# Attention beside a weight product: the first scores moved to the end of the product's first half, seven slots a unit

## The chip, the core and the metric

One core of a Trainium2 chip runs the program. TensorE (PE) multiplies, VectorE (DVE), ScalarE (ACT) and GpSimd (POOL) work element by element, and SyncE (SP) issues most of the DMAs. Each engine takes its own instructions strictly in the order in which they stand in the program and stops at the first one whose inputs are not there. The metric is the device time of one execution in microseconds.

## What is computed

The reference is a chunked attention followed by two gated feed-forward layers, all in float32:

```python
# per head, for each chunk of 32 queries: 8 memory keys + 16 left + 32 + 8 right = 64 keys
scores = scale * q_c @ k_full.T ;  a = softmax(scores) ;  out = a @ v_full
x = out as 3072 tokens x 512
h = ((x @ w1) * (x @ w2)) @ w3          # 512 -> 1024 -> 1024
x = h @ w_out                            # 1024 -> 512
y = ((x @ w_a) * (x @ w_b)) @ w_out2     # 512 -> 1536 -> 512
```

The kernel multiplies `w3 @ w_out` once, ahead of everything else, so that the second and third lines need one product with the result.

## The kernel before

**The weights' product.** Half 0 and half 1 (the loop `for half in range(2)`) each fill four PSUM banks (`wps`, 128x512) from eight terms k = 0..7. The order is k = 0..5 with the four banks m in turn, then for each bank its k = 6 and k = 7: 32 matmuls a half. The weights arrive as raw 64-bit halves in 1 MB loads (`w3a`, eight of them, for half 0; `w3b`, four, with two terms each, for half 1), which wait for one of four buffers. `w_tick` moves one load a step further: ACT scales it (`w_scale`, two instructions), one tick later DVE adds its halves (`w_sum`, two instructions) and frees the buffer, and the next load is issued. A finished bank is copied out by `w_evict` (one ACT and one DVE instruction); half 1 uses the same four banks, so its first matmul in bank m waits for the DVE instruction of `w_evict` of bank m of half 0.

**The attention.** It is cut into 16 units u of 192 tokens. A unit's stages are functions: `a_k`, `a_q`, `a_v` (loads, into `kraw`, `q`, `v`, one buffer each; `a_v` is 12 DMAs), `a_keys` (two DVE copies, `kraw` to `kw`), `a_scores` (96 small matmul records, `sc`), `a_max` (DVE), `a_exp(0..3)` (four ACT instructions each, tile `t`), `a_norm(0..1)` (two small DVE instructions and a POOL multiply), `a_trans` (8 transposes, `pt`), `a_pt` (ACT copy `p`), `a_pv` (96 matmul records, `xp`), `a_x` (ACT and DVE write the tokens into `xt`). Three units (`UA`) fill the first 512-token tile `xt`.

**The order.** A table STAGES gives each stage of a unit a slot number, and unit u starts at slot 9u. `attn_slot()` writes out the stages of the next slot. It is called between the matmuls of the weights' product (after every second matmul), and in `between()`, which stands after each half step of a tile. A tile of 512 tokens has 24 such gaps: 8 steps with two halves (`psA`, `psB`, 12 matmuls each) and 4 output blocks (`psY`). `NEED[i]` is the slot up to which the stages must be written before tile i; `between()` spreads the slots evenly over the first 22 gaps, which gives 27 slots for three units. `between()` also calls `w_tick`, as long as w1/w2 loads (`in_w`, 0.5 MB each, three buffers) are in work. Before the first tile, `a_k(0)` and `a_q(0)` are written behind the first tick, ahead of the fifth 1 MB load; `a_v(0)` and `a_keys(0)` at k = 2; and unit 0's scores at k = 3.

What follows the attention (six tiles, then the second layer with lines 790 to 814) is not touched.

Of the kernel before, what the change touches and what calls it, by code (L numbers as in the profile page):

```python
# [7 lines left out]
F32 = mybir.dt.float32  # L8
# [9 lines left out]
GQ = 96  # L18
# [3 lines left out]
KEYS = NMEM + LEFT + CHUNK + RIGHT  # L22
NC = GQ // CHUNK
TT = 512
NT1 = B * S // TT
NU = B * NG * 2
NE = 2
NA = B * NG // NE
# [17 lines left out]
def tile_attention_moe(  # L46
# [123 lines left out]
    def a_max(u):  # L170
# [8 lines left out]
        t = att.tile([GQ, NH, 2, KEYS], F32, tag="t", bufs=1, name="t")  # L179
# [66 lines left out]
    def a_x(u):  # L246
# [18 lines left out]
    NS_U = 9  # L265
    STAGES = (
        (9, a_x),
        (7, a_pt),
        (8, a_pv),
        (6, a_trans),  # L270
        (1, a_max),
        (2, a_exp(0)),
        (2, a_exp(1)),
        (3, a_norm(0)),
        (3, a_exp(2)),
        (3, a_exp(3)),
        (4, a_norm(1)),
        (0, a_scores),
        (2, lambda u: a_q(u + 1)),
        (7, lambda u: a_keys(u + 1)),  # L280
        (8, lambda u: a_k(u + 2)),
        (10, lambda u: a_v(u + 1)),
    )
    todo = {}
    for u in range(NA):
        for j, (s, stage_of) in enumerate(STAGES):
            todo.setdefault(NS_U * u + s, []).append((j, u, stage_of))
    acount = [0]
    NEED = [NS_U * (-(-TT * (i + 1) // (NE * GQ)) - 1) + 10 for i in range(NT1)]

    def attn_slot(n=1):
        for _ in range(n):
            s = acount[0]
            if s >= NEED[-1]:
                return
            acount[0] += 1
            for _, u, stage_of in sorted(todo.get(s, []), key=lambda x: x[:2]):
                stage_of(u)
# [221 lines left out]
    wz = att.tile([GQ, 2, TT], F32, tag="t", bufs=1, name="wz")[:, 0]  # L520
# [9 lines left out]
    for i in range(3):  # L530
        w_tick()
        if i == 0:
            a_k(0)
            a_q(0)

# [7 lines left out]
    for half in range(2):  # L543
        banks = [psd.tile([P, 512], F32, tag="d", name="wps") for _ in range(4)]
        for k, m in order:
# [9 lines left out]

            if half == 0:
                if k == 2 and m == 1:
                    a_v(0)
                if k == 2 and m == 3:
                    a_keys(0)  # L560
                    a_k(1)
                if m == 1 or k == 7 and m == 3:
                    w_tick()
                attn_slot(int(k > 2))
            else:
                if k < 6:
                    if m == 3:
                        w_tick()
                    attn_slot(1 + (m == 3 and k < 4))
                else:  # L570
                    if m % 2 == 1:
                        w_tick()
                    if m < 2:
                        attn_slot()
            if k == 7 and m > 0:
                w_evict(half, m - 1)
# [427 lines left out]
```

## Time and profile before

| | us |
|---|---|
| median of 3 runs | 1092.21 (1090.35 to 1092.55) |
| the profiled execution | 1088.65 |
| its span | 1086.9 |
| PE busy | 1063.5 |

The profile belongs to one execution with a time of its own; a difference worked out in it is set against the median. A row of a timeline reads: start, duration, engine, line, operation, tile written<-tiles read, and in brackets how long the engine was idle before and what released it. "issue" stands for idle time in which the engine waited for nothing that the profile shows. Two records of a 128x512 matmul are one float32 matmul of the weights' product.

### The profile page before, as it was taken

What the parts mean: (1) busy time and instruction counts of PE and PEld (TensorE: products, weight loads), DVE (VectorE), ACT (ScalarE), POOL (GpSimd) and SP (SyncE); (2) the same over time, 40 slices, a digit from 0 to 9 for tenths busy, and PEclk for the clock granted to TensorE, in tenths of its full rate; (3) what the DMA queues carried; (4) which work ended last, traced back from release to release, by engine and by line L of the source; (5) the groups of instructions that cost most, each with busy time, mean ns of one, the idle gap of its engine ahead of it and who ended that gap; (6) DMA issues with size and microseconds to landing.
All of it is one profiled execution on the core that took longest, in us unless ns stands there. A gap on an engine that the chain in (4) does not pass through costs nothing.

```text
span 1086.9 us, 18651 instructions
## 1 busy us (share of the span) xinstructions
PE 1063.5 (98%) x7442; PEld 851.3 (78%) x7442; DVE 453.3 (42%) x763; ACT 440.8 (41%) x1153; POOL 236.0 (22%) x228
## 2 busy tenths in 40 slices
PE   7999999999999999999999999999999999999998
PEld 2546778888878878888878888888888888888886
DVE  4667742435444434336653433452223253222220
ACT  5768754435545535445344333322222232222220
POOL 0011221212212213212122232103223301322210
PEclk9899999999999999999999999999999999999999
DMA  9977646355544634246545555515433442443311
GB/s 326 299 168 194 180 142 170 111 157 152 172 131 142 186 116 141 98 153 254 194 169 181 178 198 206 173 58 192 147 136 137 164 154 107 162 178 136 136 40 39
DMA packets 85575, 173.23 MB, mean 159 GB/s; under 512 B 7920, under 2 KB 48880, under 8 KB 79600
## 3 DMA queue, kind: packets, MB, share of 16 engines
q1 hardware_dynamic: 74912, 105.93, 31.7%
q0 software_dynamic: 10368, 66.06, 16.8%
q8 instruction: 59, 0.97, 0.4%
q14 instruction: 28, 0.23, 0.1%
q10 hardware_dynamic: 208, 0.04, 0.0%
HBM read 138.45 MB, written 33.55 MB: 158 GB/s over the span
## 4 chain that ended last, share of the span: by engine, by line
PE 91%; DMA 4%; ACT 2%; DVE 1%; issue 1%; POOL 0%; SPq 0%; ACTq 0%
PE ps L790 31%; PE ops L90 18%; PE psY L90 12%; PE psB L90 12%; PE psA L90 12%; PE xp L90 3%; DMA raw<-in_w3a 2%; PE sc L90 2%; PE wps L90 1%; ACT t L191 1%; DMA raw<-in_w 1%; DMA raw<-in_w3b 1%; PE pt L219 1%; ACT raw L351 0%; DMA id_sb<-in_ident 0%
## 5 line engine op out<-in xcount | busy, mean ns | idle before, releaser
L790 PE MATMUL ps<-x,w 128*128 128x512 f32 x1512 | 348.7, 389 | 0.3 <-ACT tmp L802 0.3
L790 PEld LDWEIGHTS ps<-x,w 128*128 128x128 f32 x1512 | 283.6, 188 | 60.1 <-ACT tmp L802 1.4
L807 DVE TENSOR_TENSOR tmp<-ps,tmp 128x512 f32<-128x512 f32 x108 | 74.6, 691 | 260.6 <-PE ps L790 230.6
L90 PE MATMUL psB<-xt,w 128*128 128x512 f32 x576 | 141.4, 394 | 0.0
L90 PE MATMUL psA<-xt,w 128*128 128x512 f32 x576 | 140.2, 392 | 0.0
L609 POOL TENSOR_TENSOR g<-gv,g 128x512 fp32r<-128x512 f32 x48 | 68.7, 1432 | 319.2 <-ACT g L608 296.7
L90 PE MATMUL psY<-g,wo 128*128 128x512 f32 x576 | 136.4, 395 | 0.0
L802 ACT ACTIVATE tmp<-ps 128x512 f32<-128x512 f32 x108 | 64.4, 597 | 157.5 <-PE ps L790 147.0
L90 PEld LDWEIGHTS psY<-g,wo 128*128 128x128 f32 x576 | 108.4, 190 | 22.9
L90 PEld LDWEIGHTS psB<-xt,w 128*128 128x128 f32 x576 | 107.9, 189 | 22.7
L90 PEld LDWEIGHTS psA<-xt,w 128*128 128x128 f32 x576 | 107.4, 188 | 23.0 <-issue 0.5
L674 POOL DMA_DIRECT2D w<-wc x72 | 39.7, 552 | 373.3 <-PE ps L790 373.2
L90 PE MATMUL ops<-wo,g 128*128 128x512 f32 x504 | 118.6, 389 | 0.0
L90 PEld LDWEIGHTS ops<-wo,g 128*128 128x128 f32 x504 | 94.6, 188 | 19.6
L813 ACT ACTIVATE g<-tmp 128x512 fp32r<-128x512 f32 x66 | 40.7, 633 | 140.2 <-DVE tmp L812 140.2
L814 POOL TENSOR_TENSOR g<-tmp,g 128x512 fp32r<-128x512 f32 x66 | 84.0, 1291 | 20.8 <-ACT g L813 19.8
L191 ACT ACTIVATE t<-sc,mx 96x64 f32<-96x64 f32 x256 | 75.2, 316 | 6.9 <-DVE mx L183 6.9
L607 DVE TENSOR_TENSOR gv<-psB,av 128x512 f32<-128x512 f32 x48 | 33.1, 690 | 91.2 <-PE psB L90 66.7
L90 PE MATMUL ops<-fo,g 128*128 128x512 f32 x288 | 68.2, 389 | 0.0
L90 PEld LDWEIGHTS ops<-fo,g 128*128 128x128 f32 x288 | 54.1, 188 | 11.2
L608 ACT ACTIVATE g<-gv 128x512 fp32r<-128x512 f32 x48 | 30.5, 636 | 74.5 <-DVE gv L607 74.4
L90 PE MATMUL wps<-w_f 128*128 128x512 f32 x128 | 59.4, 612 | 1.1 <-issue 0.8
(65 smaller groups left out, 907.5 us busy)
## 6 DMA issues: line engine op xcount, KB each, us to landing
w<-wc POOLq DMA_DIRECT2D x36, 1024.0 KB, 6.9
w<-wc POOLq DMA_DIRECT2D x36, 768.0 KB, 5.0
wc<-co SPq DMA_DIRECT2D x84, 256.0 KB
raw<-in_wab SPq DMA_DIRECT2D x24, 512.0 KB
v<-in_vw SPq DMA_DIRECT2D x96, 112.0 KB
kraw<-in_kt SPq DMA_DIRECT2D x32, 256.0 KB
raw<-in_w SPq DMA_DIRECT2D x16, 512.0 KB
raw<-in_w3a SPq DMA_DIRECT2D x6, 1024.0 KB
```

The lines of the kernel that those rows point to most:

```text
L90: nc.tensor.matmul(o, lhsT=l, rhs=r, start=first, stop=last)
L191: nc.scalar.activation(t[:, a, r, :], sc[:, r, a, :], AF.Exp, bias=mx[:, r, a : a + 1], scale=SCALE, accum_out=sm[:, a, r : r + 1],)
L219: nc.tensor.transpose(pt[:, a // 4, a % 4, :], t[:, a].rearrange("p r k -> p (r k)"), id_sb)
L607: nc.vector.tensor_tensor(gv, psB[:, :TT], av, ALU.mult)
L608: nc.scalar.activation(g2[:, 0, :], gv, AF.Copy)
L609: nc.gpsimd.tensor_tensor(g2[:, 1, :], gv, g2[:, 0, :].bitcast(F32), ALU.subtract)
L674: nc.gpsimd.dma_start(out=t[:, c0:c1].bitcast(F32), in_=src[:, c0:c1])
L790: nc.tensor.matmul(ps, lhsT=w[:, i, a, k, :], rhs=xs[i][:, b, k, :], start=first and n == 0, stop=n == 5, skip_group_check=not first,)
L802: nc.scalar.activation(z, ps, AF.Copy)
L807: nc.vector.tensor_tensor(z, ps, y, ALU.add)
L813: nc.scalar.activation(g2[:, 0, :], z, AF.Copy)
L814: nc.gpsimd.tensor_tensor(g2[:, 1, :], z, g2[:, 0, :].bitcast(F32), ALU.subtract)
```

## The change

The scores of unit 0 move from k = 3 to bank 1's k = 7, the loads of its keys and queries behind the eighth 1 MB load (`(k, m) == (1, 3)`), and its `a_keys`, with unit 1's key load, to bank 0's k = 7. `BASE` replaces 9u: units 1 and 2 start at slots 4 and 9, and from unit 3 (slot 19) on a unit has seven slots, so that a tile's 22 gaps take 21 or 22 slots for three units (14 for two), one in each. The tile `t` gets two buffers. Inside a unit, transpose and ACT copy stand in one slot (from unit 3 on) and the `xp` matmuls one slot later. Bank m-1 is evicted ahead of the tick and the slot at the same place, not behind them.

```diff
--- before.py
+++ after.py
@@ -176,7 +176,7 @@
                 a_edge(sc, slice(0, CHUNK), hs, NMEM, NMEM + LEFT)
             if g == NG - 1:
                 a_edge(sc, slice(GQ - CHUNK, GQ), hs, KEYS - RIGHT, KEYS)
-        t = att.tile([GQ, NH, 2, KEYS], F32, tag="t", bufs=1, name="t")
+        t = att.tile([GQ, NH, 2, KEYS], F32, tag="t", bufs=2, name="t")
         mx = att.tile([GQ, 2, NH], F32, tag="mx", bufs=2, name="mx")
         sm = att.tile([GQ, NH, 2], F32, tag="sm", bufs=2, name="sm")
         nc.vector.tensor_reduce(mx, sc, axis=mybir.AxisListType.X, op=ALU.max)
@@ -262,31 +262,38 @@
         for src, dst in parts:
             split_lo(dst[:, 1], src, dst[:, 0])
 
-    NS_U = 9
-    STAGES = (
-        (9, a_x),
-        (7, a_pt),
-        (8, a_pv),
-        (6, a_trans),
-        (1, a_max),
-        (2, a_exp(0)),
-        (2, a_exp(1)),
-        (3, a_norm(0)),
-        (3, a_exp(2)),
-        (3, a_exp(3)),
-        (4, a_norm(1)),
-        (0, a_scores),
-        (2, lambda u: a_q(u + 1)),
-        (7, lambda u: a_keys(u + 1)),
-        (8, lambda u: a_k(u + 2)),
-        (10, lambda u: a_v(u + 1)),
-    )
+    BASE = [0, 4, 9]
+    BASE += [BASE[-1] + 10 + 7 * i for i in range(NA - UA)]
     todo = {}
+
+    def at(s, *stages):
+        todo.setdefault(s, []).extend(stages)
+
     for u in range(NA):
-        for j, (s, stage_of) in enumerate(STAGES):
-            todo.setdefault(NS_U * u + s, []).append((j, u, stage_of))
+        early = u < UA
+        t = 6 if early else 5
+        for s, stage_of in (
+            (t, a_trans),
+            (t + early, a_pt),
+            (t + 1 + early, a_pv),
+            (0, a_scores),
+            (1, a_max),
+            (2, a_norm(0)),
+            (3, a_norm(1)),
+            (1, a_exp(0)),
+            (1, a_exp(1)),
+            (2, a_exp(2)),
+            (2, a_exp(3)),
+            (t + 2 + early, a_x),
+            (1, lambda u: a_q(u + 1)),
+            (t + 2 + early, lambda u: a_v(u + 1)),
+        ):
+            at(BASE[u] + s, (stage_of, u))
+        if u > 0:
+            at(BASE[u] - 2, (a_keys, u))
+            at(BASE[u] - 1, (a_k, u + 1))
+    NEED = [BASE[-(-TT * (i + 1) // (NE * GQ)) - 1] + 8 + 2 * (i == 0) for i in range(NT1)]
     acount = [0]
-    NEED = [NS_U * (-(-TT * (i + 1) // (NE * GQ)) - 1) + 10 for i in range(NT1)]
 
     def attn_slot(n=1):
         for _ in range(n):
@@ -294,7 +301,7 @@
             if s >= NEED[-1]:
                 return
             acount[0] += 1
-            for _, u, stage_of in sorted(todo.get(s, []), key=lambda x: x[:2]):
+            for stage_of, u in todo.get(s, []):
                 stage_of(u)
 
     plan = []
@@ -517,7 +524,7 @@
 
     w_load()
     warm = psd.tile([P, 512], F32, tag="d", name="warm")
-    wz = att.tile([GQ, 2, TT], F32, tag="t", bufs=1, name="wz")[:, 0]
+    wz = att.tile([GQ, 2, TT], F32, tag="t", bufs=2, name="wz")[:, 0]
     nc.vector.memset(wz, 0.0)
     for _ in range(5):
         mm(warm[:GQ], wz[:, :GQ], wz, True, True)
@@ -529,10 +536,6 @@
     w_load()
     for i in range(3):
         w_tick()
-        if i == 0:
-            a_k(0)
-            a_q(0)
-
     def w_evict(half, m):
         w = wsm[4 * half + m] = w_new(wpool, "wo")
         nc.scalar.activation(w[:, 0, :], banks[m], AF.Copy)
@@ -553,27 +556,30 @@
             if k < 6 and m % 2 == 0 or k == 6:
                 continue
 
+            if k == 7 and m > 0:
+                w_evict(half, m - 1)
             if half == 0:
-                if k == 2 and m == 1:
+                if m == 1 or k == 7 and m == 3:
+                    w_tick()
+                if (k, m) == (1, 3):
+                    a_k(0)
+                    a_q(0)
+                if (k, m) == (2, 3):
                     a_v(0)
-                if k == 2 and m == 3:
+                if (k, m) == (7, 0):
                     a_keys(0)
                     a_k(1)
-                if m == 1 or k == 7 and m == 3:
-                    w_tick()
-                attn_slot(int(k > 2))
+                elif k == 7:
+                    attn_slot()
             else:
                 if k < 6:
                     if m == 3:
                         w_tick()
-                    attn_slot(1 + (m == 3 and k < 4))
+                    attn_slot()
                 else:
                     if m % 2 == 1:
                         w_tick()
-                    if m < 2:
-                        attn_slot()
-            if k == 7 and m > 0:
-                w_evict(half, m - 1)
+                    attn_slot()
         w_evict(half, 3)
     del pairs["f"]
     wo_f.clear()
```

On PE, from the warm-up to the first tile's first half step. `wps` is the weights' product, `sc`, `pt`, `xp` are the attention's. Before:

```order
L90 MATMUL wps<-w_f 128x512 x14
L90 MATMUL sc<-kw,q 32x64 x48
L90 MATMUL wps<-w_f 128x512 x12
L219 MATMUL pt<-id_sb,t 128x96 x8
L90 MATMUL wps<-w_f 128x512 x4
L90 MATMUL xp<-p_339,v 64x32 x48
L90 MATMUL wps<-w_f 128x512 x2
L90 MATMUL sc<-kw,q 32x64 x48
L90 MATMUL wps<-w_f 128x512 x8
L219 MATMUL pt<-id_sb,t 128x96 x8
L90 MATMUL wps<-w_f 128x512 x4
L90 MATMUL xp<-p_543,v 64x32 x48
```

Now:

```order
L90 MATMUL wps<-w_f 128x512 x28
L90 MATMUL sc<-kw,q 32x64 x48
L90 MATMUL wps<-w_f 128x512 x8
L90 MATMUL sc<-kw,q 32x64 x48
L90 MATMUL wps<-w_f 128x512 x4
L219 MATMUL pt<-id_sb,t 128x96 x8
L90 MATMUL wps<-w_f 128x512 x4
L90 MATMUL xp<-p_464,v 64x32 x48
L90 MATMUL wps<-w_f 128x512 x2
L90 MATMUL sc<-kw,q 32x64 x48
L90 MATMUL wps<-w_f 128x512 x2
L219 MATMUL pt<-id_sb,t 128x96 x8
```

Unit 0's `sc` stands behind 28 matmuls in place of 14, `sc` of unit 1 behind 8 more of them, and unit 0's `pt` and `xp` come behind both.

On ACT, at the end of half 0. `raw_210` before and `raw_204` now are the second `w3b` load, `raw_276` and `raw_215` the third; `wo<-wps` is an eviction; `t,sm<-sc,mx` are unit 0's exponentials. Before:

```order
L191 ACTIVATE t,sm<-sc,mx 96x64 x16
L350 ACTIVATE raw_194<-raw_194 128x1024
L351 ACTIVATE raw_194<-raw_194 128x1024
L350 ACTIVATE raw_210<-raw_210 128x1024
L351 ACTIVATE raw_210<-raw_210 128x1024
L225 ACTIVATE p_339<-pt 128x768
L538 ACTIVATE wo<-wps 128x512 x2
L350 ACTIVATE raw_276<-raw_276 128x1024
L351 ACTIVATE raw_276<-raw_276 128x1024
```

Now:

```order
L541 ACTIVATE wo<-wps 128x512
L357 ACTIVATE raw_204<-raw_204 128x1024
L358 ACTIVATE raw_204<-raw_204 128x1024
L541 ACTIVATE wo<-wps 128x512
L191 ACTIVATE t,sm<-sc,mx 96x64 x8
L541 ACTIVATE wo<-wps 128x512
L357 ACTIVATE raw_215<-raw_215 128x1024
L358 ACTIVATE raw_215<-raw_215 128x1024
L191 ACTIVATE t,sm<-sc,mx 96x64 x8
L541 ACTIVATE wo<-wps 128x512
```

The exponentials of unit 0 stood ahead of the `w3b` loads; they now stand behind two of them, with the evictions of banks 1, 2 and 3 between.

On PE, in the output blocks of the first tile, from unit 5's `xp` on. Before:

```order
L90 MATMUL xp<-p_1746,v 64x32 x48
L90 MATMUL sc<-kw,q 32x64 x48
L90 MATMUL psY<-g_909,wo 128x512 x3
L90 MATMUL psY<-g_991,wo 128x512 x3
L90 MATMUL psY<-g_1057,wo 128x512 x3
L90 MATMUL psY<-g_1123,wo 128x512 x3
```

Now:

```order
L90 MATMUL xp<-p_1724,v 64x32 x48
L90 MATMUL psY<-g_1289,wo 128x512 x3
L90 MATMUL psY<-g_1363,wo 128x512 x3
L90 MATMUL psY<-g_1402,wo 128x512 x3
L90 MATMUL psY<-g_1507,wo 128x512 x3
L90 MATMUL sc<-kw,q 32x64 x48
```

The 96 records of `xp` and the 96 of the next unit's `sc` followed each other directly; twelve large matmuls now stand between.

## Rows read from the trace of the kernel before

**Rows 1.** The page, busy time: engine, us, share, instructions.

```profile
PE 1063.5 (98%) x7442; PEld 851.3 (78%) x7442; DVE 453.3 (42%) x763; ACT 440.8 (41%) x1153; POOL 236.0 (22%) x228
```

**Rows 2.** Waits of PE in the span: total us, times, longest.

```profile
PE sc L90 <- DVE kw L145: 5.7, 1, 5.7
PE sc L90 <- issue: 4.8, 4, 1.8
PE xp L90 <- ACT p L225: 3.7, 2, 2.2
```

**Rows 3.** Timeline of PE up to unit 1's `sc`.

```profile
15.96 5.42 PE L90 MATMUL wps<-w_f 128*128 128x512 f32 x12 [0.24 <-DVE w_f L356]
...
27.11 1.95 PE L90 MATMUL sc<-kw,q 64*32 64x64 f32 x96 [5.73 <-DVE kw L145]
...
53.31 0.44 PE L90 MATMUL sc<-kw,q 64*32 64x64 f32 x23 [0.46 <-issue]
```

**Rows 4.** Chain that ended last, first `psB`: start us, us, what.

```profile
94.72 2.72 PE psB L90 x12
```

**Rows 5.** Timeline of ACT, the 1 MB loads' first scaling and unit 0's exponentials.

```profile
15.85 1.14 ACT L350 ACTIVATE raw<-raw 128x1024 f32<-128x1024 f32 x1 [1.20 <-DMA raw<-in_w3a]
...
22.72 1.10 ACT L350 ACTIVATE raw<-raw 128x1024 f32<-128x1024 f32 x1 [4.68 <-DMA raw<-in_w3a]
...
25.21 1.15 ACT L350 ACTIVATE raw<-raw 128x1024 f32<-128x1024 f32 x1 [0.35 <-DMA raw<-in_w3a]
...
30.56 1.16 ACT L350 ACTIVATE raw<-raw 128x1024 f32<-128x1024 f32 x1 [0.68 <-DMA raw<-in_w3a]
...
32.67 0.29 ACT L191 ACTIVATE t<-sc,mx 96x64 f32<-96x64 f32 x1
...
37.00 0.34 ACT L191 ACTIVATE t<-sc,mx 96x64 f32<-96x64 f32 x1
...
38.80 1.15 ACT L350 ACTIVATE raw<-raw 128x1024 f32<-128x1024 f32 x1 [1.37 <-DMA raw<-in_w3b]
```

**Rows 6.** Groups by line and shape, 30 to 95 us: busy, mean ns, idle before.

```profile
L539 DVE TENSOR_TENSOR wo<-wps,wo 128x512 fp32r<-128x512 f32 x8 | 5.4, 688 | 6.1 <-ACT wo L538 6.1
L538 ACT ACTIVATE wo<-wps 128x512 fp32r<-128x512 f32 x8 | 4.6, 592 | 3.8 <-PE wps L90 3.8
L182 DVE TENSOR_REDUCE mx<-sc 96x16 f32<-96x1024 f32 x3 | 3.7, 1217 | 0.6 <-PE sc L90 0.5
L144 DVE COPY kw<-kraw 128x1344 f32<-128x1344 f32 x3 | 2.6, 851 | 0.0
```

**Rows 7.** Timeline of SP, four issues.

```profile
50.85 0.27 SPq L130 DMA_DIRECT2D v<-in_vw  x1
...
59.84 0.32 SPq L131 DMA_DIRECT2D v<-in_vw  x1
...
65.26 0.36 SPq L335 DMA_DIRECT2D raw<-in_w  x1
...
75.34 0.32 SPq L131 DMA_DIRECT2D v<-in_vw  x1
```

**Rows 8.** Stretches: us, busy of each engine, granted TensorE clock, DMA share, GB/s.

```profile
94.72:121.70 26.98, 24.79 (x284) 20.18 (x284) 23.40 (x37) 21.80 (x63) 6.76 (x5) 0.94 0.70 197
...
309.00:327.00 18.00, 16.27 (x249) 13.28 (x249) 5.87 (x13) 4.41 (x10) 0.00 (x0) 0.91 0.45 147
```

**Rows 9.** Timeline of PE in the first tile.

```profile
114.15 2.38 PE L90 MATMUL xp<-p,v 64*64 64x32 f32 x96 [1.49 <-ACT p L225]
116.46 4.19 PE L90 MATMUL psB<-xt,w 128*128 128x512 f32 x12
```

**Rows 10.** Timeline of PE, three later `sc` groups that stop.

```profile
144.94 0.82 PE L90 MATMUL sc<-kw,q 64*32 64x64 f32 x59 [0.79 <-issue]
...
319.79 0.44 PE L90 MATMUL sc<-kw,q 64*32 64x64 f32 x23 [1.73 <-issue]
...
400.02 0.52 PE L90 MATMUL sc<-kw,q 64*32 64x64 f32 x27 [1.83 <-issue]
```

## The prediction

> **What bounds the kernel now.** I read the page's busy times first, then the waits of PE, then PE's timeline, then the timelines of those that PE waits for. PE is busy 1063.5 us of a span of 1086.9 [rows 1], and the change takes no work from it: it can win from 23.4 us of idle time and from work that runs at the lower clock. Three waits stand out [rows 2]: 5.7 us before unit 0's `sc`, where the copies of its keys come late, 4.8 us of stops inside `sc` that nothing shown explains, and 3.7 us before `xp`. Three stretches matter: the start up to unit 1's `sc`, which ends at 53.75 (53.31 + 0.44 [rows 3]); from there to the first tile's `psB` at 94.72 [rows 4], by which time unit 3's `sc` is done too; and the first tile.
>
> **Start: what becomes faster.** The 5.73 us wait at 27.11 goes, and with it the slow `sc` behind it (1.95 us) [rows 3]. Two loads of 1 MB are scaled 2.49 us apart (22.72, 25.21 [rows 5]), as they land. With `kraw` and `q` behind all eight, the fifth to eighth land some 4.4 us earlier (15.85 to 22.72 is 6.87, less 2.49), so the eighth at about 26 for 30.56 before [rows 5]. From 15.96 on PE does its next 20 matmuls at 0.9 us at most (six, in twelve records, took 5.42 us [rows 3]) without a wait, then `sc` (1.2) and the last four of half 0: done at about 38.7. Before, half 0 ended at about 51.9, with unit 0's `pt` and `xp` (some 2.2 us) in it.
>
> **Start: what is late next.** Half 1's bank 1 needs bank 1 of half 0 evicted, and in the new ACT order that eviction stands behind the scaling of the second `w3b` load, which has to land first. Keys and queries land 4.4 us after the eighth load (30.4), the first `w3b` load at 32.9. Ahead of the second come unit 0's twelve `v` loads. Before, the eighth `w3a` and the first `w3b` load, with the same twelve between, were 8.24 us apart (30.56, 38.80 [rows 5]), and unit 1's keys, which shared the end of that stretch, no longer do. That gives 41 without a credit for this and 38 if it counts fully; I take 39. From there ACT, DVE and PE follow each other: scaling 2.2, eviction 0.6 + 0.7 [rows 6], so bank 1 goes on at 42.5, where PE stands since 39.6; maximum 1.7 (its reduction is 1.22 [rows 6]), eight exponentials 2.35 (0.29 each: sixteen start between 32.67 and 37.00 [rows 5]), eviction 1.3, so bank 2 goes on at 48; scaling 2.2, exponentials 2.35, eviction 1.3: bank 3 at 53.1. DVE has one more thing ahead of that eviction: unit 1's `kw` copies (0.85 [rows 6] + 0.25), which wait for `kraw` behind two more `w3b` loads (till 44) and three `in_w` loads. In the program a load's semaphore is used again by the eighth load behind it, whose issue waits for the landing, so the `v` issues tell landings: 50.85 the last `w3b` load, 59.84 the next keys, 9.0 us [rows 7]. That gives 53.0, copies till 54.1, bank 3 at 54.8; at full rate throughout 3 us less. I take 54 for bank 3, then 0.9 + 1.2 and 0.4 for the lower clock after so much idling: unit 1's `sc` ends at 56.5 for 53.75, **+2.7** (bounds +0.5 and +5). By then PE has done four matmuls more and a `pt` and an `xp` less.
>
> The Trainium skill (DMA: Bandwidth & Descriptors, Rules for kernel authors) advises to issue a DMA early and to wait for it late; sending unit 1's keys behind six more loads goes against that. Before, the keys were 9.0 us behind the last `w3b` load too and made no one wait; by the page they will now, at the worse bound, and the sum would be -2.4 for the -4.7 below.
>
> **From unit 1's `sc` to `psB`.** Before: 40.97 us. After, counted from the end T of that `sc`: ACT does maximum, exponentials, one 0.5 MB scaling, exponentials and `p` in 8.4 us, one more than PE needs to get there; `xp` of unit 0 ends at T + 10. Only then is the single `v` buffer free. Unit 1's `v` loads follow an `in_w` load and unit 3's keys on SP; before, the same row of issues took 10.1 us (65.26 to 75.34 [rows 7]), to which I add 2.4 for the landing, about the middle of nothing and of the 4.8 us after which SP went on behind that 0.5 MB load: T + 22.8. PE is there at T + 18.7 and waits **4.1 us**, since `a_pv` stands three slots behind the `v` issue, where it had seven. Then `xp`, six matmuls, `pt`, four matmuls, with 1 us for the lower clock, to T + 34.8; unit 2's `v` is there by then. `xp` 1.6, `xt` 2.0, `psA` 2.7, `sc` 1.2: T + 42.3. That is **+1.3** (bounds -2 and +5).
>
> **First tile.** 94.72 to 121.70 holds 22.4 us of matmuls at full clock (seven half steps of 2.72 [rows 4], `pt` 0.7, `xp` 1.6, `sc` 1.1) and takes 27.0 at a granted 0.94 of the clock [rows 8]: 4.6 are lost, 1.49 of it in front of `xp`, whose copy stands on ACT behind scalings that wait for their loads; the half step after it takes 4.19 us [rows 9]. Now the copy of `p` follows its transposes in the same slot; walking ACT through its new order, `p` ends 0.6 us after PE wants it. **-4.0** (bounds 0 and -4.6).
>
> **Stops inside `sc`.** At 319.79 and 400.02 PE has stood 1.73 and 1.83 us in the middle of an `sc` that follows its `xp` directly: 192 records in 2.7 us [rows 10]. Of the four such pairs two stop so long; of the twelve others two stop, for 0.46 [rows 3] and 0.79 [rows 10]. The change leaves no such pair. From `psB` on, 4.35 us of stops and 1.6 us at half clock behind the first long one (granted 0.91 over 18 us [rows 8]) become about 1.3, two stops of the small kind: **-4.7** (bounds -6 and 0).
>
> The Trainium skill (Runtime: NRT & Kernel Launch, Instruction fetch mechanics) calls the cost of fetching the next block of instructions mostly hidden. By that page a stop of 1.8 us can't be the code's loading, and more room between the groups would buy nothing: the sum would be 0.0 and not -4.7. The rows show the stops, and not their cause.
>
> **Nothing gained or lost.** The second buffer of `t` costs space alone. The evictions ahead of the tick save less than the wait for the load takes. The ends of the tiles keep their order.
>
> **Sum.** +2.7 + 1.3 - 4.0 - 4.7 = -4.7. The profiled execution takes 1088.65, so it would take 1084.0; on the median, 1092.21 - 4.7 = **1087.5**. The median stands 3.6 above the profiled execution, and I keep that distance.
>
> **Rivals.** (1) *The stops stay.* If they hang on nothing that the spacing changes, -4.7 falls away: 1092, no change. For it: two groups that are not adjacent stop too. Against it: the long ones are adjacent. (2) *ACT stays behind in the first tile,* which now has all of unit 3's exponentials behind `psA`: -4.0 falls away, 1091.5; with the start at its worse bound 1094. (3) *Slower: `p` does not get through one gap.* In most units `xp` now follows `pt` by 12 matmuls (2.7 us), where nine units had 24. If ACT is held by a scaling that waits for its load, as at 114.15, PE waits 1.5 and loses 2 more in the slow work behind [rows 9], 3.5 a unit. Two such units give +2.3, three +5.8 (1098): from two on it is slower. Against it: the four units of before that had 12 didn't wait.
>
> **How the numbers follow.** A change below 0.2% (2.2 us) can't be told from none here. The forecast, 1081 to 1090, has a chance of 0.53; rival 1 0.17, rival 2 0.13, rival 3 0.17. Faster takes the forecast but for its upper end, 0.50; no change that end and most of rivals 1 and 2, 0.30; slower what is left of these and rival 3, 0.20. The range runs from 1081 (start and stops at their better bounds) to 1096, where rival 3 has between two and three waits.
>
> **What would show it.** The wait before the first `sc` is gone; PE stands in half 1 in front of banks 1, 2 and 3 on DVE's evictions, 12 us or so in all; `xp` of unit 1 waits some 4 us on a `v` load; the first tile's `psB` starts at 98 to 99 for 94.72, but unit 4's `sc` ends about as late as before; few stops over 1 us in `sc`. Wrong would be the start if bank 3 goes on before 51 or after 58, the tiles if `xp` waits for `p` in more than one of them.

## The result, and the profile of the changed kernel

The changed kernel is slower: 1095.88 us (median of 15 runs, 1092.02 to 1099.47) for 1089.5 (1085.13 to 1092.63), a ratio of 1.0063 with a 95% interval of 1.0043 to 1.0083. Forecast were 1087.5 and a gain, on a time before of 1092.21 from three runs; the fifteen runs here put the same kernel at 1089.5. The profiled span is 1094.7 us for 1086.9, 7.8 more, and splits at the same three points that the prediction used (ends are start plus duration in PE's timeline; for the kernel before, the last two points are the prediction's 94.72 and 121.70):

| stretch | before | predicted | after | difference |
|---|---|---|---|---|
| up to the end of unit 1's `sc` | 53.75 | +2.7 | 59.54 | +5.8 |
| from there to the first `psB` | 40.97 | +1.3 | 47.00 | +6.0 |
| first tile, `psB` to the end of unit 4's `sc` | 26.98 | -4.0 | 26.68 | -0.3 |
| from there to the end | 965.2 | -4.7 | 961.5 | -3.7 |

The waits of PE over the whole span (us, times, longest) show what took the place of [rows 2]: the 5.7 in front of unit 0's `sc` and the 4.8 of stops inside `sc` have become 11.1 for evictions, some new waits before `xp`, and one stop.

```profile
PE wps L90 <- DVE wo L542: 11.1, 3, 4.2
PE xp L90 <- ACT p L225: 2.0, 1, 2.0
PE xp L90 <- DMA v<-in_vw: 1.9, 2, 1.0
PE xp L90 <- issue: 1.8, 2, 1.1
...
PE sc L90 <- issue: 1.0, 1, 1.0
```

PE's timeline (start, us, what, in brackets the idle time before and its releaser) answers to [rows 3] and [rows 9]. Half 0 ends with 34.46 + 3.70, as predicted; then come the three banks, unit 1's `sc`, the wait for `v`, the slow stretch behind it, and the first tile's wait for `p`:

```profile
34.46 3.70 PE L90 MATMUL wps<-w_f 128*128 128x512 f32 x8
...
44.50 2.08 PE L90 MATMUL wps<-w_f 128*128 128x512 f32 x2 [4.21 <-DVE wo L542]
50.04 2.07 PE L90 MATMUL wps<-w_f 128*128 128x512 f32 x2 [3.46 <-DVE wo L542]
55.58 2.08 PE L90 MATMUL wps<-w_f 128*128 128x512 f32 x2 [3.47 <-DVE wo L542]
57.59 1.95 PE L90 MATMUL sc<-kw,q 64*32 64x64 f32 x96
...
82.03 2.13 PE L90 MATMUL xp<-p,v 64*64 64x32 f32 x68 [0.96 <-DMA v<-in_vw]
85.30 0.63 PE L90 MATMUL xp<-p,v 64*64 64x32 f32 x10 [1.14 <-issue]
85.86 8.40 PE L90 MATMUL wps<-w_f 128*128 128x512 f32 x12
...
106.54 3.01 PE L90 MATMUL psB<-xt,w 128*128 128x512 f32 x12
...
125.86 2.96 PE L90 MATMUL xp<-p,v 64*64 64x32 f32 x96 [1.96 <-ACT p L225]
128.75 3.35 PE L90 MATMUL psB<-xt,w 128*128 128x512 f32 x12
132.03 1.19 PE L90 MATMUL sc<-kw,q 64*32 64x64 f32 x96
...
330.52 0.44 PE L90 MATMUL sc<-kw,q 64*32 64x64 f32 x22 [0.98 <-issue]
```

Stretches of the same run (us, then busy time of PE, PE's weight load, DVE, ACT and POOL, granted clock, DMA share, GB/s). Around the wait for `v` and after it the granted clock is 0.64 and 0.63: most of it at the lower of its two levels (1.2 of 2.4 GHz). The first tile still runs at 0.94, as in [rows 8].

```profile
80.01:85.86 5.85, 3.62 (x94) 3.19 (x94) 0.25 (x2) 1.47 (x3) 1.04 (x1) 0.64 0.96 251
85.86:94.10 8.24, 8.24 (x13) 3.42 (x13) 2.68 (x4) 2.44 (x4) 0.00 (x0) 0.63 0.54 167
...
106.54:133.20 26.66, 24.70 (x290) 20.43 (x285) 20.87 (x34) 20.68 (x61) 6.61 (x5) 0.94 0.70 192
```

ACT's timeline answers to [rows 5]: the second `w3b` load is scaled at 41.15 after 4.63 us of waiting, the first eviction of the second half's path stands behind it at 43.14, the next behind eight exponentials at 48.65, the last at 53.48. In the first tile ACT waits 1.90 us for a weight load and gets to `p` at 124.98.

```profile
41.15 1.10 ACT L357 ACTIVATE raw<-raw 128x1024 f32<-128x1024 f32 x1 [4.63 <-DMA raw<-in_w3b]
...
43.14 0.58 ACT L541 ACTIVATE wo<-wps 128x512 fp32r<-128x512 f32 x1
...
53.48 0.64 ACT L541 ACTIVATE wo<-wps 128x512 fp32r<-128x512 f32 x1
...
115.13 0.67 ACT L357 ACTIVATE raw<-raw 128x512 f32<-128x512 f32 x1 [1.90 <-DMA raw<-in_w]
...
124.98 0.82 ACT L225 ACTIVATE p<-pt 128x768 f32<-128x768 f32 x1
```

### The profile page after: what moved, and what is told of

It reads as the page before. It is cut to its first block, busy times and chain, and to the rows that moved or that the text cites. A ratio compares the mean times of both kernels' runs of the same rounds, so it can differ in the third digit from the quotient of the medians.

```text
span 1094.7 us, 18642 instructions
## 1 busy us (share of the span) xinstructions
PE 1068.9 (98%) x7442; PEld 851.3 (78%) x7442; DVE 459.9 (42%) x763; ACT 441.4 (40%) x1153; POOL 234.8 (21%) x228
## 4 chain that ended last, share of the span: by engine, by line
PE 85%; DVE 1%; ACT 1%; issue 0%; POOL 0%; ACTq 0%; DVEq 0%
PE ps L796 31%; PE ops L90 18%; PE psY L90 12%; PE psB L90 11%; PE psA L90 10%; PE xp L90 2%; PE sc L90 1%; PE pt L219 1%; ACT t L191 0%; DVE dec L363 0%; DVE x L100 0%; DVE tmp L650 0%; ACT w L399 0%; POOL t L208 0%; ACT x L97 0%
## 5 line engine op out<-in xcount | busy, mean ns | idle before, releaser
L90 PEld LDWEIGHTS psA<-xt,w 128*128 128x128 f32 x576 | 107.2, 188 | 22.8 <-issue 0.2
L191 ACT ACTIVATE t<-sc,mx 96x64 f32<-96x64 f32 x256 | 75.6, 319 | 22.8 <-DVE mx L183 22.8
L90 PE MATMUL wps<-w_f 128*128 128x512 f32 x128 | 65.5, 658 | 12.5 <-DVE wo L542 11.1
L90 PEld LDWEIGHTS wps<-w_f 128*128 128x128 f32 x128 | 25.1, 207 | 45.4 <-issue 25.3
```

What stands on the lines that cost most here:

```text
L90: nc.tensor.matmul(o, lhsT=l, rhs=r, start=first, stop=last)
L191: nc.scalar.activation(t[:, a, r, :], sc[:, r, a, :], AF.Exp, bias=mx[:, r, a : a + 1], scale=SCALE, accum_out=sm[:, a, r : r + 1],)
```

## Experiments

Ratios are to the kernel before unless something else is named; each comes with its 95% interval. The theory, from the table above: the start loses (ACT's order around the evictions, the late `v`, the late keys), the spacing of the dense groups gains a few us, and the first tile is spoilt by loads on SP. The rival: the spacing brings nothing, or the start's loss lies in what the loads can deliver, whatever their order.

### Tiles alone: old start, new table from unit 3 on

```diff
+    BASE = [9 * min(u, UA) + 7 * max(0, u - UA) for u in range(NA)]
...
+        if u >= UA:
+            stages = (
+                (5, a_trans),
+                (5, a_pt),
+                (6, a_pv),
+                (0, a_scores),
...
```

> The kernel before with its own start (nine slots for units 0 to 2, unit 0's scores at the end of half 0) and, from unit 3 on, the order of the changed kernel (seven slots a unit, the spacing of its groups). Theory: the changed kernel's program gained 3.7 us from unit 4's scores to its end (961.5 for 965.2) and lost 11.9 us ahead of the first tile, so without the new start this one is about 3.7 us faster than before, 0.9966 of it, with fewer stops inside the scores. Rival: the 3.7 us come from the later start of the tiles (loads that are further ahead), not from the spacing; then this one is within 1 us of before.

Measured: 0.999 (0.9972 to 1.0007), no difference that can be told. The trace tells why it is less than 3.7: from the end of unit 4's `sc` on it is 960.7 us for 965.2, a gain of 4.5, and stops inside the tiles' `sc` are down to 0.24 and 0.26. But in the start a stop inside `wps` is 1.91 us for 0.82, and in the first tile `xp` now waits 4.16 us for `p` (1.49 in [rows 9]), because ACT stood 2.85 us for a weight load. ACT's timeline and PE's:

```profile
113.09 0.65 ACT L371 ACTIVATE raw<-raw 128x512 f32<-128x512 f32 x1 [2.85 <-DMA raw<-in_w]
```

```profile
117.17 2.96 PE L90 MATMUL xp<-p,v 64*64 64x32 f32 x96 [4.16 <-ACT p L225]
```

The whole is within about 1 us of before, as the rival had it, but not for its reason: by the one trace of each, the stretch with the spacing gains without the new start, and the first tile eats most of it. All thirteen kernels here that have the spacing take 960.3 to 963.8 us in that last stretch. The loss of the changed kernel is the start's.

### The start: unit 1's `v` early

```diff
-            (t + 2 + early, lambda u: a_v(u + 1)),
+            ((3, 5)[u] if u < 2 else t + 2 + early, lambda u: a_v(u + 1)),
```

Unit 1's `v` gets a buffer of its own, beside the raw weights'.

> The changed kernel, but unit 1's v is loaded early into a buffer of its own (slot 3 of unit 0), and unit 2's v behind unit 0's last use (slot 5 of unit 1). Theory: the wait of xp of unit 1 for v (0.95 + 0.96 us, then 1.14 of standing without a shown cause) and the lower clock behind it (twelve half-matmul records in 8.40 us for 5.2) are one loss; the first tile's psB starts some 5 to 6 us earlier than 106.6 and the whole is 5 to 6 us faster than the changed kernel. Rival: the lower clock comes from the three waits in half 1 and from the idle time before, not from the v wait; then only the 2 to 3 us of the wait go and the slow stretch stays.

Measured: 1.0032 (1.0016 to 1.0049), 0.3% better than the changed kernel (the intervals just overlap). The wait, the stop behind it and the slow stretch go together: the same twelve records take 5.42 us for 8.40, at a granted clock of 1.00 and with the DMA share at 0.94. The row of PE's timeline, and the stretch:

```profile
81.89 5.42 PE L90 MATMUL wps<-w_f 128*128 128x512 f32 x12
```

```profile
81.89:87.14 5.25, 5.25 (x18) 2.34 (x13) 2.68 (x4) 2.42 (x5) 1.04 (x1) 1.00 0.94 238
```

The three waits for evictions are still there (11.3 us in all), so they are not what slows that stretch, against the rival. The first `psB` starts at 101.36 for 106.54, the 5 us of the theory. Of these only some 3 arrive at the end: the first tile's `xp` waits 2.13 us for `p` and the half step behind it takes 4.62 us, and the stops in `sc` come to 2.0 us for 1.0.

### The start: unit 1's keys and queries early

```diff
                     a_k(0)
                     a_q(0)
+                    a_k(1)
+                    a_q(1)
...
                     a_keys(0)
-                    a_k(1)
```

Unit 1's `kraw` and `q` get buffers of their own.

> The changed kernel, but unit 1's raw keys and its queries have buffers of their own and are loaded directly behind unit 0's queries, ahead of all loads of the second half's weights. In the changed kernel bank 3 of half 1 goes on at 55.6, where the eviction ahead of it stands behind both ACT (53.5) and the copies of unit 1's keys (till 54.95), which landed at 53.8. Theory: ACT's row of work behind the second w3b load sets all three waits; keys sent earlier push that load back by some 4 us (1.5 MB ahead of it), so bank 1 goes on at about 48 for 44.5 and bank 3 at 57 to 59, and the whole is 0 to 4 us slower than the changed kernel. Rival: the late landing of the keys sets the third wait, as the prediction had it; then bank 3 goes on at 53 to 54 and the whole is 1 to 2 us faster.

Measured: 1.0085 (1.0057 to 1.0114), if anything slower than the changed kernel (the intervals overlap). The banks go on at 50.59, 56.12 and 60.99; the first matmuls of half 1 wait 5.20 us for their weights. The keys' copies now run at 58.15 without a wait, and the third wait is still 2.80 us of 3.47. So ACT's row sets these waits. The keys, the prediction's second reason for bank 3, account for the other 0.7: in the changed kernel ACT's eviction ends at 54.12 (53.48 + 0.64), and DVE's starts at 54.84, behind the copies. PE's timeline with the early keys, then DVE's of the changed kernel:

```profile
43.99 2.08 PE L90 MATMUL wps<-w_f 128*128 128x512 f32 x2 [5.20 <-DVE w_f L363]
50.59 2.08 PE L90 MATMUL wps<-w_f 128*128 128x512 f32 x2 [4.52 <-DVE wo L542]
56.12 2.07 PE L90 MATMUL wps<-w_f 128*128 128x512 f32 x2 [3.45 <-DVE wo L542]
60.99 2.08 PE L90 MATMUL wps<-w_f 128*128 128x512 f32 x2 [2.80 <-DVE wo L542]
```

```profile
53.90 0.86 DVE L144 COPY kw<-kraw 128x1344 f32<-128x1344 f32 x1 [1.75 <-DMA kraw<-in_kt]
...
54.84 0.68 DVE L542 TENSOR_TENSOR wo<-wps,wo 128x512 fp32r<-128x512 f32 x1
```

### The start: evictions first

```diff
-                if m == 1 or k == 7 and m == 3:
-                    w_tick()
+                if m == 1:
+                    w_tick(scales=k < 7)
...
         w_evict(half, 3)
+        if half == 0:
+            w_tick(sums=False)
```

At k = 7 the tick leaves the scaling out, which then stands behind the fourth eviction; unit 0's exponentials follow in half 1. Not shown of the edit: one more tick at k = 1 of half 1, and two places there that write out two slots at once, to make up for the slots left out at k = 7.

> The changed kernel with one thing moved at the end of the first half of the weights' product: all four evictions stand ahead of unit 0's exponentials and of the scaling of the second w3b load (that load's scaling comes directly behind the fourth eviction; one more tick early in half 1 makes up for it). Theory: the three waits of half 1 for DVE's evictions (4.2 + 3.5 + 3.5 us) come from ACT's row of work between the evictions and go; PE then stands once, in front of unit 1's scores, whose keys land at 53.8 and whose queries at 55.4: those scores end at 57 to 58 for 59.4, and the whole gains about 2 us or less over the changed kernel. Rival: the waits are the evictions' own time (PE to ACT to DVE and back); then some 2 us of wait stay in front of each bank.

Measured: 1.0035 (1.0016 to 1.0054). All three waits go, and one of 12.17 us stands in their place, in front of unit 1's `sc`, whose raw keys DVE gets at 56.38. PE's timeline and DVE's:

```profile
57.66 2.26 PE L90 MATMUL sc<-kw,q 64*32 64x64 f32 x96 [12.17 <-DVE kw L145]
```

```profile
56.38 0.86 DVE L144 COPY kw<-kraw 128x1344 f32<-128x1344 f32 x1 [7.91 <-DMA kraw<-in_kt]
```

Two waits lay over one another: ACT's row and the late keys end within 3 us of each other, and taking away one leaves the other. Unit 1's `sc` ends at 59.92 for 59.54, no gain there. What it does gain over the changed kernel (0.28% by the ratios, their intervals overlap) comes later: the first `psB` starts 1.1 us earlier, at 105.41, and the first tile takes 2.1 us less, with a wait of 1.06 us for `p`. That may be due to the extra tick or the doubled slots, which were not tried apart.

### The start: evictions first, keys and `v` early

The edits of the last three experiments together.

> The kernel above (evictions first), and unit 1's keys and queries sent directly behind unit 0's queries, and unit 1's v early into a buffer of its own. Theory: the losses of the start lay over one another (ACT's row, the late keys, the late v), and with all three away unit 1's scores end at 47 to 50 (53.75 in before, 59.35 in the changed kernel), the first tile's psB starts at 89 to 93 (94.7 and 106.6), and the whole is 8 us faster than before, less the wait for p in the first tile, which stays: 0.992 to 0.996 of before. Rival: the start is bound by what the loads can bring (the weights of the first tile); then PE waits for weights instead ahead of the first tile, psB starts no earlier than 94, and the whole is within 3 us of before.

Measured: 1.0004 (0.9989 to 1.0019): the start's loss is gone, but nothing is won over before. Unit 1's `sc` starts at 54.61 and not at 46, and the first `psB` at 96.72. Two waits are left (PE's timeline, then ACT's):

```profile
42.45 7.00 PE L90 MATMUL wps<-w_f 128*128 128x512 f32 x12 [4.31 <-DVE w_f L368]
54.61 1.95 PE L90 MATMUL sc<-kw,q 64*32 64x64 f32 x96 [5.17 <-DMA v<-in_vw]
```

```profile
54.09 0.38 ACT L196 ACTIVATE t<-sc,mx 96x64 f32<-96x64 f32 x1
```

The first is the weights that the early keys pushed back. The second is put down to a `v` load, but the last of unit 0's exponentials, which read the scores of unit 0, ends at 54.47, and in a later run (unit 3's `v` later, below) the same wait of 4.14 us is put down to them. They stand behind the scalings of two `w3b` loads on ACT. I expected 47 to 50, and the rival's "within 3 us of before" holds, though PE waits at another place than the rival said.

### The start: evictions first and `v` early, keys as in the change

> The changed kernel with evictions first and unit 1's v early, its keys and queries where the change has them (behind the second half's weights). Theory: the late keys are a loss of their own that the waits for the evictions hid: unit 1's scores start at 57 to 58 as with evictions first alone, some 3 us later than with the keys early too, and the whole is 2 to 4 us slower than with all three, 1.002 to 1.004 of before. Rival: keys early only push the weights back by what they gain; then this one equals the one with all three, 1.000 to 1.001.

Measured: 1.0029 (1.0012 to 1.0046), slower than with the keys early too by 0.25% (the intervals just overlap). Unit 1's `sc` starts at 56.27, 1.7 us later (3 were expected), after a wait of 11.80 us for its keys. So the keys' place behind six more loads does cost something once ACT's row is out of the way. Moved early alone, as above, they gained nothing.

### The first tile: unit 3's `v` three slots later

```diff
-            (t + 2 + early, lambda u: a_v(u + 1)),
+            (12 if u == 2 else t + 2 + early, lambda u: a_v(u + 1)),
```

> The changed kernel, but unit 3's v loads (twelve issues on SP) are issued three slots later. In the changed kernel a weight load of the first tile is issued at 109.3, behind those twelve and the next keys, lands at 115.05, ACT waits 1.9 us for it and is behind until p, for which xp waits 1.96 us; the half step behind that runs at the lower clock. Theory: SP's row of issues sets that; the wait for p and the slow half step go, 3 to 4 us faster than the changed kernel. Rival: the weight load is late because its buffer comes free late, not for the issues ahead of it; no change within 1 us.

Measured: 1.0041 (1.0028 to 1.0054), about 2.4 us better than the changed kernel, with intervals that overlap. In the changed kernel SP issued the twelve `v` loads from 102.37 on, then keys, and only then the weight load that ACT waited for; with the edit two weight loads go out from 102.02 on. SP's timeline of the changed kernel, then of this one, then ACT's, PE's row and the tile's stretch of this one:

```profile
102.37 0.30 SPq L130 DMA_DIRECT2D v<-in_vw  x1
...
109.32 1.02 SPq L342 DMA_DIRECT2D raw<-in_w  x2
```

```profile
102.02 2.25 SPq L342 DMA_DIRECT2D raw<-in_w  x2
...
109.31 0.33 SPq L130 DMA_DIRECT2D v<-in_vw  x1
...
115.22 7.86 SPq L342 DMA_DIRECT2D raw<-in_w  x4
```

```profile
119.86 0.67 ACT L357 ACTIVATE raw<-raw 128x512 f32<-128x512 f32 x1 [1.85 <-DMA raw<-in_w]
```

```profile
121.82 1.97 PE L90 MATMUL xp<-p,v 64*64 64x32 f32 x96 [1.33 <-ACT p L225]
```

```profile
102.00:127.90 25.90, 24.33 (x361) 19.99 (x363) 22.14 (x35) 21.50 (x62) 6.59 (x5) 1.00 0.80 225
```

The wait for `p` is 1.33 for 1.96 us, and the tile runs at a granted 1.00 for 0.94. SP's row of issues is a cause, and the edit has moved it more than removed it: ACT now waits 1.85 us for a weight load right ahead of `p`, by the order of issues and scalings the one that goes out at 115.22, directly behind the twelve `v`.

The same edit on top of evictions first, keys and `v` early:

> Evictions first, unit 1's keys, queries and v early, and unit 3's v three slots later. Theory: the losses of start and first tile are apart from one another, so this one has both gains: 3 to 4 us better than the one with the start alone, 0.988 to 0.993 of before. Rival: what is won at the start is lost again in the first tile, where the weights' row on ACT and DVE is what PE runs into; then no better than the one with the start alone.

Measured: 0.999 (0.9974 to 1.0006). That is 0.14% better than without, some 1.5 us for the 3 to 4 expected; the interval doesn't tell it from either.

### The stops: groups adjacent again

```diff
-            (0, a_scores),
+            (0 if u < 4 else -1, a_scores),
```

> The changed kernel, but from unit 4 on the scores of a unit stand in the slot right behind the product with v of the unit ahead, so that the two dense groups (192 records) follow each other on PE again, as they did four times in the kernel before. Theory: the spacing took the stops away (of four such pairs in before two stopped 1.73 and 1.83 us, in the changed kernel one group stopped 0.98); with twelve such pairs about half stop some 1.8 us and some run slowly behind it, 6 to 15 us slower than the changed kernel. Rival: the stops hang on something else; then it is within 2 us of the changed kernel.

Measured: 1.022 (1.0181 to 1.0259), some 17 us slower than the changed kernel by the two ratios and 20 by the profiled spans, more than expected. Six stops come to 15.6 us, the longest 3.61, and the work behind them runs at the lower clock. The rows are PE's waits, its timeline, the stretch behind the longest stop (granted clock 0.53), and the DMA queues from 341.50 to 342.00 (packets, MB, share): the data's queue is full, and one packet of an instruction queue is among it.

```profile
PE sc L90 <- issue: 15.6, 6, 3.6
```

```profile
344.47 0.45 PE L90 MATMUL sc<-kw,q 64*32 64x64 f32 x10 [3.61 <-issue]
344.85 10.71 PE L90 MATMUL psY<-g,wo 128*128 128x512 f32 x36
```

```profile
344.50:350.00 5.50, 5.50 (x23) 4.25 (x24) 0.00 (x0) 0.00 (x0) 0.00 (x0) 0.53 0.37 92
```

```profile
q1 hardware_dynamic: 110, 0.11, 108.4%
q8 instruction: 1, 0.02, 17.2%
```

So the spacing is what keeps PE from stopping in these pairs; nothing else of the stage table was changed. Groups that stand apart are not safe by that alone: two runs below stop 2.03 us in an `xp` and 2.20 us in an `sc` of the start.

### The stops: adjacent groups, loads elsewhere

```diff
-            at(BASE[u] - 1, (a_k, u + 1))
+            at(BASE[u] + (3 if u > 2 else -1), (a_k, u + 1))
-            (t + 2 + early, lambda u: a_v(u + 1)),
+            (9 if u > 2 else t + 2 + early, lambda u: a_v(u + 1)),
```

> The kernel with adjacent groups (each unit's scores right behind the product with v of the unit ahead), but from unit 3 on the next keys are issued four slots later and the next v two slots later, so that these loads no longer run while the two groups do. With adjacent groups PE stood 15.6 us in six places inside the scores, and in each of those stretches the DMA queues of the data were at their full share while one packet of the instruction queue stood between them (PE stopped at 340.9, the packet was served at about 341.5, PE went on at 344.5 when the data ended). Theory: a stop is code that comes late because it shares the DMA engines with the data; then the stops shrink to under a third (5 us or less) and the kernel is 8 us or more faster than with adjacent groups alone. Rival: 192 short instructions in a row outrun the code's delivery whatever else runs; then the stops stay within 4 us of 15.6.

Measured: 1.0139 (1.0107 to 1.0172), 9 us better than adjacent groups alone by the ratios; stops of 9.9 us for 15.6, six again, at nearly the same records. Both theories miss their numbers. The `sc` that stopped 3.61 us still stops 2.40, though the DMA queues are all but empty (waits, timeline, and the queues from 329.00 to 329.50):

```profile
PE sc L90 <- issue: 9.9, 6, 2.4
```

```profile
331.60 0.31 PE L90 MATMUL sc<-kw,q 64*32 64x64 f32 x7 [2.40 <-issue]
```

```profile
q8 instruction: 1, 0.02, 11.8%
q1 hardware_dynamic: 5, 0.01, 6.5%
```

PE goes on 2.2 to 2.4 us after the start of that packet here, and 2.3 to 2.9 after it with the queues full. So data beside the groups makes a stop longer, and the adjacency brings it about.

That a stop is the wait for that packet can be read from all sixteen traces together. Queue q8 carries 59 packets of 16 KB in each, for 15,047 to 15,059 recorded instructions of PE (matmuls, weight loads and semaphore instructions), some 255 a packet. Counted from the first instruction, PE crosses 58 borders, one every 256 instructions (at 192 above a multiple of 256), 928 in all. At 50 of them it stands for 0.15 us or more, in `sc`, `xp` or `wps`, and these are all of its stops put down to "issue" but one (0.31 us, in an `xp` whose `v` is late). At each of the 50 the last packet ahead is the one with the number of the border, and PE goes on 2.2 to 3.5 us after its start. The 878 other borders are crossed 2.3 us or more after the start of their packet. So a stop is the wait for the next block of PE's code, and 192 records, which are 384 instructions in 2.7 us, always hold a border. No run changed the packets themselves, and why one goes out late isn't shown.

### The stops: groups apart, the same later loads

> The changed kernel (groups apart) with the same later loads from unit 3 on; unit 3's own v stays where it was. Theory of late code: the one stop of 0.98 us goes, and nothing else is touched: 0 to 1.5 us faster than the changed kernel. Rival: loads issued later make copies of keys or products with v wait; then new waits for v or keys in the tiles, 2 us or more slower.

Measured: 1.0046 (1.0029 to 1.0062). The one stop of 0.98 is gone and no stop inside `sc` is left. But in the start, which the edit doesn't touch, the two stops inside `xp` are 2.03 and 1.21 us for 1.14 and 0.66, and a `pt` waits 2.69 us for POOL; no copy of keys waits. Whether it is faster than the changed kernel the intervals don't tell.

### Towards a better kernel

Old start, new table, unit 3's `v` one slot and unit 4's queries three slots later:

> Start of before, seven slots from unit 3 on, and unit 3's v one slot and unit 4's queries three slots later. With the old start and seven slots xp waited 4.2 us for p in the first tile, because ACT stood 2.85 us for a weight load that was issued behind unit 3's v and unit 4's queries. Theory: that wait shrinks to 1 to 2 us and the half step behind it keeps the full clock; 2 to 4 us faster than with the old order of these loads, 0.995 to 0.997 of before. Rival: the weight load is late for its buffer; then no change, 0.999.

Measured: 0.9981 (0.9962 to 0.9999). The first tile's wait for `p` is 1.28 us for 4.16, and unit 4's `sc` starts at 117.83 for 123.39 with the old order of these loads (1.3 of the 5.6 lie ahead of the tile). In the start unit 1's `sc`, two large matmuls behind an `xp`, stops for 2.20 us (0.46 in [rows 3]), which this edit doesn't touch.

That one, with the next keys four slots and the next `v` two slots later from unit 3 on:

> Start of before, seven slots from unit 3 on, unit 3's v one slot and unit 4's queries three slots later (0.9981 of before), and from unit 3 on the next keys four slots and the next v two slots later. Theory of code that comes late beside the data: the stops that are left in the tiles (0.67, 0.68, 0.22 us) shrink, about 1 us faster, 0.997 of before. Rival: keys or v now come late for their use: a wait for v or for kw in the tiles, 1.000 or more.

Measured: 0.9973 (0.9955 to 0.9991), the lowest ratio of all, and below 1 by its interval; from the one above (0.9981) and the next one (0.9988) it can't be told. No stop is left in the tiles, and PE's only waits of over 0.4 us there are 2.27 and 1.34 for `p`.

The new start with everything mended and the same later loads:

> Evictions first, unit 1's keys, queries and v early, unit 3's v three slots later, and the later loads of keys and v from unit 3 on. The one without the last part stopped 2.2 us in the scores in three places. Theory of late code: these stops go, 1 to 3 us faster than without, 0.996 to 0.998 of before. Rival: the stops stay; 0.999 as without.

Measured: 0.9988 (0.997 to 1.0005). The tiles' stops go (1.0 us is left, in the start), but the total is that of the kernel without: a `pt` waits 1.19 us for POOL instead.

## Why the prediction was wrong

**Start, +2.7: mechanism right, size wrong.** The wait before the first `sc` went, half 0 ended where it should (38.2), and PE stood before banks 1, 2 and 3 for 11.1 us ("12 us or so"). But bank 1 went on at 44.5 for 42.5: the second `w3b` load was there at 41.15, where the prediction chose 39 between "41 without a credit" and 38. The credit was wrong, and ACT, DVE and PE carried the 2 us on, so that bank 3 went on at 55.58 for 54. Another 1.5 are the bank's last two matmuls and `sc`, at 2.08 + 1.95 us for the 2.5 allowed: behind three waits in a row they ran wholly at the lower clock. The late keys held bank 3 for only 0.7 us, as the keys' run and DVE's row show. The sign that the prediction gave for a wrong start (bank 3 before 51 or after 58) didn't show: the loss sat behind bank 3 as much as ahead of it.

**From unit 1's `sc` to `psB`, +1.3: this step failed most.** The `v` load came when the walk said (T + 22.5; the walk's terms add up to that, though it wrote T + 22.8). PE waited 1.9 us for it and not 4.1, since `xp` ran on each piece as it landed. What followed was mis-sized: 1 us for the lower clock, where twelve records alone took 3.0 us more than the 5.42 that they take without the wait, and a stop of 1.14 and one of 0.66 in `xp` that were not thought of. The run with `v` early takes 6.8 us off this stretch (40.2 for 47.0). The price was in the trace of before: [rows 9] has a half step of 4.19 us behind a wait of 1.49. I used it for a rival and not for this wait.

**First tile, -4.0: failed.** This is what the second rival (0.13) forecast, ACT behind in the first tile, though for another reason: it named unit 3's exponentials, and the trace shows a load. The copy of `p` did follow its transposes in the same slot, but the walk of ACT's order took the loads as landed. A weight load stood on SP behind twelve `v` issues that the new table puts there; ACT waited 1.90 us for it and then had no idle time up to `p`. PE lost 1.96 of waiting, and `xp` and the half step behind it took 2.96 and 3.35 us, 1.7 more than the 1.61 and 3.01 of undisturbed ones; the tile kept its 0.94.

**Stops, -4.7: right.** By the one trace of each kernel, the last stretch is 3.7 us shorter in the changed kernel and 4.5 with the old start (1.4 to 4.9 over the thirteen kernels with the spacing); twelve adjacent pairs cost 17 to 20 us. The first rival (stops stay) falls.

The Trainium skill (Runtime: NRT & Kernel Launch, Instruction fetch mechanics) calls a crossing to the next block of code "mostly hidden". The traces agree for 878 of 928 crossings and not for 50, the longest of 3.61 us. So the prediction took too much from that page where it said that a stop of 1.8 us can't be the code's loading; it forecast the gain from the rows in spite of it, without knowing the cause.

**Third rival** (slower, because `p` does not get through one gap): `xp` waited for `p` in one tile only, so slower came from elsewhere. That the way up to the first `psB` could lose 11.8 us was none of the cases; its two bounds of +5 and +5 were both passed, and the range's upper end (1096) was set for another reason. That the 1095.88 lies below it is luck: on the prediction's base of 1092.21 the measured ratio would have given 1099.

The Trainium skill (DMA: Bandwidth & Descriptors, Rules for kernel authors) advises to issue early and wait late. Here the loads share one stretch in which the DMA queues are nearly full (a share of 0.94 to 0.96 around 80 to 87 us), and what goes earlier pushes something back: keys early cost 0.2% alone, which can't be told from nothing, and gained 0.25% with the other two waits gone. `v` early, into a buffer of its own, gained 0.3%. The prediction had put the page's case at the start's worse bound (+5, a sum of -2.4); the start took +5.8, but the late keys were 0.7 of it.

**What stays open.** Whether a new start can be better than the old one: with everything mended it equals the kernel before (0.9990 and 0.9988, both intervals with 1 in them), against 0.9973 for the old start with the same later loads; the waits that are left are for the weights' landing and for ACT. Why evictions first also help in the first tile. Why the packet with PE's next block sometimes goes out so late.

## What to carry to other kernels

A wait taken from one engine is only worth the distance to the next thing that is late, so walk the second and third arrival too, and walk each queue with the issues that the edit puts ahead of the ones that matter: here twelve small loads, some 0.35 us each on SP, spoilt the tile that the edit was meant to mend. Charge every wait of PE with the slow work behind it, from a row of the same trace. Put large matmuls between groups of very short ones: twelve took nearly all of the stops away here, two did not. A stop with no releaser in the middle of a group is worth a count of PE's instructions up to it.

## What was not expected of the hardware

- The lower clock after a wait lasts unevenly: behind waits for the same `v` loads the next twelve records took 8.40 us in the changed kernel (3.05 us of waits and stop), 6.80 with unit 3's `v` later (2.33 us; nothing in the program differs up to there), 7.45 with the later loads (3.78 us), and 5.42 without the wait. So the idle time alone doesn't tell the price.
- 192 short matmul records in a row stop PE in six of twelve places for 1.7 to 3.6 us beside loads, and for 1.1 to 2.4 us with those loads moved away, the longest with the DMA queues all but empty; with twelve large matmuls between the two groups one stop of 0.98 us in `sc` is left.
- All 50 stops stand at the border between two blocks of 256 instructions of PE, each brought by a 16 KB packet, and end 2.2 to 3.5 us after the start of that packet.
